# Block attention and a channel mixer on one core: in five of 32 pairs of heads, DMA transposes of halved probabilities in place of TensorE's

## The chip, the cores and the metric

The kernel runs on one core of a Trainium2 chip. Its engines work side by side, each through its own instructions in order: TensorE (PE; its weight loads are shown as PEld), VectorE (DVE), ScalarE (ACT), GpSimd (POOL) and SyncE (SP), which issues the DMA transfers. The metric is the device time of one execution in microseconds (us); less is better.

## What is computed

Eight batches of eight heads, 576 positions, 64 channels a head. Attention is masked by blocks of 64 positions, and its output goes through a mixer:

```python
scores = scale * np.matmul(q, k.transpose(0, 1, 3, 2))
mask = block_i >= block_j                    # blocks of 64 positions
attn = np.exp(scores - max) / (sum + 1e-09)
x = np.matmul(attn, v)                       # heads side by side: (8, 576, 512)
u = x + (x.transpose(0, 2, 1) @ U @ V).transpose(0, 2, 1)      # U: 576 x 32, V: 32 x 576
out = u + np.maximum(u @ w_ch1, 0.0) @ w_ch2                   # 512 x 2048, 2048 x 512
```

## The kernel before

Two heads are worked on together, so there are 32 pairs, four to a batch. The 576 rows of a head's scores lie in five blocks of rows: block 0 has 64 rows, blocks 1 to 4 have 128, and block i needs 128 i + 64 columns of keys. A pair is worked off in two sets of five such blocks (`scores(p, s, ...)` with s = 0 and 1; which block of which head belongs to which set is told by `job`). For each set PE makes the scores in PSUM (L1262), DVE finds the negative largest of each row (L1287), and ACT writes the exponentials to the tiles `p0_` to `p4_` in SBUF and their sums to `ss` (L1298). There are four tiles of each kind, taken by the number of the head.

`normalise` follows: DVE sums and inverts (L1311, L1312), and POOL multiplies the exponentials by the inverse in place (L1319). It also copies three small corners into neighbouring tiles.

The value product needs the probabilities with keys on the partitions, so `transpose` turns them on PE in squares of 128x128 in float32 (L1373), with the identity or a matrix that swaps the two halves (`swap`) as the other operand. The results go to PSUM and are copied from there to `pw` or `spare` by ACT (L1346), or, for one part in four from head 12 on, by DVE (L1344). `apply_v` (L1394) multiplies by V in float32: the queries lie in two groups of 256 and 320 columns (`g` = 1 and 0), with five and three blocks of keys; the two heads of a pair write the upper and lower 64 partitions of one bank. ACT copies the result to `xt`. `mix` then makes u of the pair (L1426, L1452, L1480), and DMA stores it in `u_d`.

The feed-forward part of the first 768 of the 2048 hidden channels is worked off in chunks of 288 positions, `ffn_chunk`: float32 numbers are split into a high and a low half-precision part, and three products (high by high, low by high, high by low) make one (L729 and L754). ACT and DVE copy its results out of two banks `bf`. These products run between those of the attention. The other 1280 channels come after the last pair, in `block_products` (L978).

All instructions are handed to `Plan` as tasks with an engine, a planned length, a priority, and what they read and write. `Plan.issue` plays the engines through with these planned lengths, always starting the ready task of lowest priority number on a free engine, and writes the instructions in that order. Attention of pair p has priorities around 2000 p (its scores some 2000 lower), feed-forward products 1e6 and up, and the copies that serve them -1. So PE takes a feed-forward product whenever, by the plan, no product of a pair is ready. The planned length of each task is varied by up to 2% with its number in the list, so that tasks added in one place also move later ones. On the chip each engine keeps the order that was written and waits by semaphores. A DMA is planned to land `DL` = 3000 ns after its issue.

SP issues every DMA, in the order of the plan: q and k of a pair (`raw`, L1210), V (`vr`, L1230), weights (`st`), u (`u_d`, `ur`) and the feed-forward results (`o_d`).

Of the kernel before, what the change touches and what calls it, by code (L numbers as in the profile page):

```python
# [189 lines left out]
class Plan:  # L190
# [140 lines left out]
def attention_then_mixer(  # L331
# [446 lines left out]
    def block_products():  # L778
# [29 lines left out]
        def at(x, *i):  # L808
            return lambda: first()[x][(slice(None), *i)]

        scored = after(*raw_r, xs, *usf.parts, *vf.parts)

        def weights(slots, by, sc, whole, room, split):

# [339 lines left out]
    ut_r = [b.split(2) for b in ring(ap, 1, [P, S], F32, "ut")]  # L1154
    ust = buf(ap, [P, 5, 2 * R], F32R, "ust").split(2)
    v3 = buf(ap, [3 * R, S], F32R, "v3").split(2)
    usf = buf(ep, [P, 5, R], F32, "usf").split(2)
    vf = buf(ep, [R, S], F32, "vf").split(2)
    xs = buf(ep, [P, 5, P], F32, "xs")


    for j in range(4):
# [142 lines left out]
    def normalise(p, s, pr):  # L1305
        slot = (2 * p + s) % 4
        ss, rv = ss_r[slot], rv_r[slot]

        def inverse():

            nc.vector.tensor_reduce(out=rv.ap, in_=ss.ap, op=ALU.add, axis=AX.X)  # L1311
            return nc.vector.reciprocal(rv.ap, rv.ap)  # L1312

        add("DVE", 274, pr, inverse, ss.parts, rv.parts)

        def scaled(out, x, iv, w, reads, to):
            add(
                "POOL", 255 + 0.85 * w, pr,
                lambda: nc.gpsimd.tensor_scalar(out=out, in0=x, scalar1=iv, scalar2=1.0, op0=ALU.mult, op1=ALU.mult),  # L1319
                reads, [to],  # L1320
            )

        def corner(q, h):
            r, n = rv_r[(2 * p + q) % 4], [i for _, i in job(p)].index(3)
            pt, to = pt_r[3][h % PB[3]], pt_r[4][h % PB[4]]
            scaled(to[0:64, 4 * P : 4 * P + 64], pt[64:P, 3 * P : 3 * P + 64], r[64:P, n : n + 1], 64, [r.parts[n], pt], to)

        for n, (x, i) in enumerate(job(p)):
            h = 2 * p + (s, 1 - s)[x]
            w, pt = P * i + 64, pt_r[i][h % PB[i]]  # L1330
            if i == 0:
                to = pt_r[1][h % PB[1]]
                scaled(to[0:64, P : P + 64], pt[0:64, 0:64], rv[0:64, n : n + 1], 64, [rv.parts[n], pt], to)
# [14 lines left out]
    def transpose(h, g, part, pr):  # L1348

        js = BLOCKS[g][part]  # L1350
        bank, span = Buf(pool=banks_p(h // 2)), _span(g, js)
        n = span.stop - span.start


        moves = []
        for j in js:
            for i in range(1, 5):
                q0 = max(P * i - 64, 0)
                a, b = max(q0, _first(g, j)), min(P * i + 64, QS[g + 1])
                if a < b and not (i == j == 3):  # L1360
                    c = _at(g, j).start - span.start + a - _first(g, j)
                    half = b - a < P
                    left = half and c + P > 512
                    moves.append((not half, i, j, swap if half and i and not left else ident, c - 64 if left else c))
        moves.sort(key=lambda m: m[0])

        def products():
            for _, i, j, perm, a in moves:
                to = bank[:, a : a + P]
                if i == j == 1 or j == 4:  # L1370
                    x, y = ((_at(g, n).start - span.start) // 64 for n in ((1, 0) if j == 1 else (3, 4)))
                    to = bank[:, :].rearrange("p (x c) -> p x c", c=64)[:, x : y + 1 : y - x, :]
                nc.tensor.transpose(out=to, in_=pt_r[i][h % PB[i]][:, j * P : (j + 1) * P], identity=perm.ap)  # L1373

        cost = 109 * len(moves)
        pts = [pt_r[i][h % PB[i]] for i in sorted({m[1] for m in moves})]
        pw = pw_of(h)[g]
        b = pw.parts[part]
        add("PE", cost, pr, products, pts, [bank], hold=[b])
        copy((g, part) in VEC and h >= 2 * VP, n, pr, lambda: pw[:, span], lambda: bank[:, :n], [bank], [b])  # L1380

    def apply_v(p, pr):
        xt, vr = xt_r[p % 2], vr_r[p % 2]
        pw = [[pw_of(2 * p + s)[g] for s in range(2)] for g in range(2)]
        bank = [Buf(pool=banks_p(p)) for _ in range(2)]
        n = [QS[g + 1] - QS[g] for g in range(2)]
        whole = [vr, *(y for g in pw for x in g for y in x.parts)]
        order = Buf()

        def products(g):  # L1390
            for j in range(NK[g]):
                x = max(P * j - QS[g], 0)
                for s in range(2):
                    nc.tensor.matmul(  # L1394
                        bank[g][64 * s : 64 * s + 64, x : n[g]], vr[:, 5 * s + j, :], pw[g][s][:, _at(g, j)],
                        start=(j == 0), stop=(j == NK[g] - 1),
                    )
# [128 lines left out]
    for p in range(NH // 2):  # L1526
        pr = 2000.0 * p
        if p + 1 < NH // 2:
            load_qk(p + 1, max(pr - LA, 1.0))
        for s in range(2):  # L1530
            scores(p, s, pr + 10 + 20 * s - (SL if p < NPAIR else SL2))
            normalise(p, s, pr + 30)
        for g in (1, 0):
            for h in (2 * p, 2 * p + 1):
                for part in range(2):
                    transpose(h, g, part, pr + 40 + 10 * (1 - g))
        apply_v(p, pr + 60)
        if p + 1 < NH // 2:
            load_v(p + 1, pr + 1000)
        mix(p, pr + (MX[1] if p % NPAIR == NPAIR - 1 else MX[0]))  # L1540
        if p == min(WH, NH // 2 - 1):
            gate = Buf()
            gate.writers = [len(plan.tasks) - 1]
            first_w2(lambda: wa, wab, lambda n: WPB + WP1 * n, 0, [gate])
            first_w1(lambda: wa, wab, lambda n: WP2 + WP3 * n, 1, [gate])
            first_w2(lambda: wa, wab, lambda n: WP4 + WP3 * n, 1, [gate])
# [55 lines left out]
```

## Time and profile before

| | before |
|---|---|
| time, median of three runs | 1076.9 us (1075.48 to 1077.45) |
| time of the profiled execution | 1076.24 us |
| its span, first to last instruction | 1074.4 us |
| granted clock | 1.000 |
| last value product of the attention | between 550 and 600 us |
| PSUM copies of the transposed probabilities and of `xt` on ACT (L1346) | 115.8 us, 268 instructions |
| scaling of the probabilities on POOL (L1319) | 183.5 us, 384 instructions |

The span runs from the first to the last instruction; the profiled execution's own time has 1.8 us around it. Busy time is given per engine; matmuls overlap in the pipeline, so that one of 288 columns is shown as 0.29 us long although the next starts 0.12 us after it. The time that a product costs is therefore read from the distance of starts, not from the length of one. The two parts of the table's last rows are whole lines over the span.

### The profile page before, as it was taken

The numbers are of one execution on the slowest core, as the hardware profiler recorded it, in microseconds if no ns is written. First come the engines' busy times: TensorE is split into PE (matmuls) and PEld (weight loads), VectorE is DVE, ScalarE is ACT, GpSimd is POOL, SyncE is SP. The second block draws the span as 40 slices with busy tenths as digits, with TensorE's granted clock in tenths as the row PEclk, the third lists the DMA queues.
The fourth block names the chain that finished last, engine by engine and source line by source line (L and its number), as shares of the span: only waits on it lengthen the run. The fifth ranks groups of instructions, "written<-read, shape, count | busy, mean of one in ns | idle before, by whom it ended". The sixth has DMA issues, their size and how long they took to land.

```text
span 1074.4 us, 25473 instructions
## 1 busy us (share of the span) xinstructions
PE 1065.3 (99%) x9676; PEld 845.8 (79%) x9676; DVE 850.3 (79%) x1799; ACT 650.7 (61%) x1674; POOL 346.3 (32%) x624
## 2 busy tenths in 40 slices
PE   9999999999999999999999999999999999999998
PEld 7678867888787888888877777777777777777776
DVE  5879987887764665778856643999898989999998
ACT  6888777766766667577585542545454545454553
POOL 4744436556545455365376460000000000000000
PEclk9999999999999999999999999999999999999999
DMA  4453635453433241444222422040404031313111
GB/s 146 136 175 121 201 107 186 137 174 116 130 103 101 82 131 63 151 132 160 89 80 74 127 59 75 1 126 9 133 13 122 18 116 32 103 37 98 41 50 45
DMA packets 68266, 107.37 MB, mean 100 GB/s; under 512 B 6896, under 2 KB 50928, under 8 KB 68144
## 3 DMA queue, kind: packets, MB, share of 16 engines
q1 hardware_dynamic: 68144, 105.75, 31.8%
q8 instruction: 76, 1.25, 0.5%
q14 instruction: 46, 0.38, 0.1%
HBM read 76.23 MB, written 29.49 MB: 98 GB/s over the span
## 4 chain that ended last, share of the span: by engine, by line
PE 93%; ACT 3%; DVE 2%; POOL 1%; issue 1%; DMA 0%; ACTq 0%; POOLq 0%; DVEq 0%
PE bb L978 38%; PE bf L754 13%; PE bf L729 12%; PE ba L1373 8%; PE ba L1394 8%; PE bw L1262 5%; PE bq L1262 3%; ACT p L1298 2%; PE ba L1426 2%; PE ba L1452 1%; PE ba L1480 1%; PE bf L1560 1%; POOL p L1319 1%; POOL w1l L831 0%; PE bf L1120 0%
## 5 line engine op out<-in xcount | busy, mean ns | idle before, releaser
L1319 POOL TENSOR_SCALAR p<-p,rv 64x64 f32<-64x64 f32 (+4 forms) x384 | 183.5, 490 | 111.1 <-DVE rv L1312 35.3
L978 PE MATMUL bb<-ph,w2h 128*128 128x288 f16 x560 | 151.1, 286 | 0.0
L978 PE MATMUL bb<-ph,w2l 128*128 128x288 f16 x560 | 151.1, 286 | 0.0
L978 PE MATMUL bb<-ph,w1l 128*128 128x288 f16 x560 | 148.8, 286 | 0.0
L978 PE MATMUL bb<-ph,w1h 128*128 128x288 f16 x560 | 148.8, 286 | 0.0
L900 ACT CAST ph<-hb 128x576 f16<-128x576 f32 x144 | 84.3, 589 | 83.1 <-PE bb L978 82.0
L978 PEld LDWEIGHTS <-w1h 128*128 128x128 f16 x1120 | 109.3, 98 | 28.0
L978 PEld LDWEIGHTS <-w2h 128*128 128x128 f16 x1120 | 109.3, 98 | 27.9
L978 PE MATMUL bb<-pl,w2h 128*128 128x288 f16 x560 | 123.7, 286 | 0.0
L1287 DVE TENSOR_REDUCE mx<-bw 128x1 f32<-128x576 f32 (+2 forms) x192 | 76.2, 436 | 50.1 <-PE bw L1262 49.2
L978 PE MATMUL bb<-pl,w1h 128*128 128x288 f16 x560 | 114.5, 286 | 0.0
L754 PE MATMUL bf<-hh,w2h 128*128 128x288 f16 x384 | 110.3, 287 | 0.4 <-DVE hl L737 0.4
L754 PE MATMUL bf<-hh,w2l 128*128 128x288 f16 x384 | 110.0, 286 | 0.6 <-DVE w2l L543 0.6
L754 PE MATMUL bf<-hl,w2h 128*128 128x288 f16 x384 | 109.9, 286 | 0.0
L1373 PE MATMUL ba<-ident,p 128*128 128x128 f32 x668 | 102.2, 276 | 0.0
L1298 ACT ACTIVATE p<-bw,mx 128x192 f32<-128x192 f32 (+2 forms) x192 | 92.5, 489 | 13.9 <-DVE mx L1287 12.0
L1262 PE MATMUL bw<-raw 64*64 64x288 f32 (+4 forms) x896 | 97.0, 346 | 0.4 <-ACT p L1298 0.3
L902 DVE TENSOR_TENSOR pl<-hb,ph 128x576 f16<-128x576 f32 x144 | 91.2, 650 | 1.5
L729 PEld LDWEIGHTS <-w1h 128*128 128x128 f16 x768 | 74.2, 98 | 19.9 <-issue 2.3
L1262 PE MATMUL bq<-raw 64*64 64x384 f32 (+1 forms) x496 | 89.7, 470 | 0.1
L754 PEld LDWEIGHTS <-w2h 128*128 128x128 f16 x768 | 75.1, 98 | 18.5 <-ACT w2h L539 0.2
L1373 PEld LDWEIGHTS ba<-ident,p 128*128 128x128 f32 x668 | 76.8, 141 | 5.6 <-issue 1.6
(193 smaller groups left out, 2386.5 us busy)
## 6 DMA issues: line engine op xcount, KB each, us to landing
raw<-in_qk_dram SPq DMA_DIRECT2D x31, 576.0 KB, 3.9
o_d<-ot SPq DMA_DIRECT2D x72, 144.0 KB, 1.8
vr<-in_v_dram SPq DMA_DIRECT2D x32, 320.0 KB, 3.0
ur<-u_d SPq DMA_DIRECT2D x64, 144.0 KB, 2.3
wr<-o_d SPq DMA_DIRECT2D x32, 288.0 KB, 3.1
out_dram<-wr SPq DMA_DIRECT2D x31, 288.0 KB, 2.3
st<-in_w_dram SPq DMA_DIRECT2D x16, 512.0 KB, 4.2
u_d<-ut SPq DMA_DIRECT2D x28, 288.0 KB, 2.1
```

The costliest lines, as they stand in the source:

```text
L729: nc.tensor.matmul(ps[:, :T], w()[wn][:, k, fs], m[k].ap, start=(i == 0), stop=(i == len(ops) - 1))
L754: nc.tensor.matmul(ps[:, :T], w()[wn][:, f, ms], hs[f][x].ap, start=(i == 0), stop=(i == len(ops) - 1))
L900: add("ACT", _act(n * T, True), E, lambda: nc.scalar.copy(h.ap[:, :n, :], x[0]()), [x[1]], [h])
L902: "DVE", _dve(n * T), E, lambda: nc.vector.tensor_sub(l.ap[:, :n, :], x[0](), h.ap[:, :n, :]), [x[1], h], [l],
L978: nc.tensor.matmul(bank[:, i, :T], x()[:, w(k)], p.ap[:, k, :], start=first and n == 0, stop=last and n == len(ops) - 1)
L1262: nc.tensor.matmul(o, raw[r, 64 * n : 64 * n + 64], raw[r, S + k0 : S + k1], start=True, stop=True)
L1287: lambda i=i, n=n: nc.vector.tensor_reduce(out=mx[: P if i else 64, n : n + 1], in_=view(i), op=ALU.max, axis=AX.XY if i == 4 else AX.X, n ...
L1298: return nc.scalar.activation(out.rearrange("p (j k) -> p j k", j=2) if i == 4 else out, view(i), AF.Exp, bias=mx[:rows, n : n + 1], accum ...
L1319: lambda: nc.gpsimd.tensor_scalar(out=out, in0=x, scalar1=iv, scalar2=1.0, op0=ALU.mult, op1=ALU.mult),
L1373: nc.tensor.transpose(out=to, in_=pt_r[i][h % PB[i]][:, j * P : (j + 1) * P], identity=perm.ap)
L1394: nc.tensor.matmul(bank[g][64 * s : 64 * s + 64, x : n[g]], vr[:, 5 * s + j, :], pw[g][s][:, _at(g, j)], start=(j == 0), stop=(j == NK[g] ...
L1426: nc.tensor.transpose(out=ps[:, i, :], in_=xt[:, j * P : j * P + rows], identity=ident.ap)
```

## The change

For the pairs 11, 15, 19, 23 and 27 (`XP`), two functions take the place of `normalise`, `transpose` and `apply_v`:

- `halve` scales the probabilities by 2^15 times the inverse sum and splits them into a high and a low half-precision part, side by side in one tile `hl16` for each kind of block. For blocks 0, 1 and 4, ACT makes the high part with the scaling in it (L1383) and DVE the low one; for blocks 2 and 3 (`XG`), POOL scales in place, ACT casts (L1379) and POOL subtracts. DMA transposes (`dma_start_transpose`, L1402) carry them into `turned`, keys on the partitions: one for blocks 2 and 4, two for the others, so eight a set and 16 a pair. There is one `hl16` tile of each kind, used by both sets, so that the second set's halves wait until the first set's transposes have read theirs. A transpose is planned with 600 ns on SP and a landing 8000 ns after (`XI`, `XD`).
- `apply_x` finds a power of two that brings V near a fixed size (DVE, with one transpose on PE), scales V on POOL, splits it into `vh` and `vl` on ACT and POOL, and multiplies in three half-precision passes (high by high, low by high, high by low): 48 products with a weight load each (L1434). ACT copies the result to `xt` with the inverse scale.

The tiles `turned` share their memory with three tiles that only the first four pairs use (`usf`, `vf`, `xs`).

```diff
+XP = (11, 15, 19, 23, 27)
+XI, XD = 600, 8000
+XG = (2, 3)
...
+    hl16 = [buf(ep, [P, 2, P * (i + 1)], F16, f"hl16_{i}") for i in range(5)]
+    vh, vl = (buf(ep, [P, 10, D], F16, x) for x in ("vh", "vl"))
...
+    def halve(p, s, pr):
...
+            if i in XG:
+                add(
+                    "POOL", 255 + 0.85 * w, pr,
+                    lambda x=x, iv=iv: nc.gpsimd.tensor_scalar(out=x, in0=x, scalar1=iv, scalar2=1.0, op0=ALU.mult, op1=ALU.mult),
+                    [rv.parts[n]], [pt],
+                )
+                add("ACT", _act(w, True), pr, lambda hi=hi, x=x: nc.scalar.copy(hi, x), [pt], [both])
+                add("POOL", 60 + 2.2 * w, pr, lambda hi=hi, lo=lo, x=x: nc.gpsimd.tensor_sub(lo, x, hi), [pt, both], [both])
+            else:
+                add(
+                    "ACT", _act(w, True) + 105, pr, lambda hi=hi, x=x, iv=iv: nc.scalar.activation(hi, x, AF.Copy, scale=iv),
+                    [rv.parts[n], pt], [both],
+                )
+                add(
+                    "DVE", 60 + 1.3 * w, pr,
+                    lambda hi=hi, lo=lo, x=x, iv=iv: nc.vector.scalar_tensor_tensor(
+                        out=lo, in0=x, scalar=iv, in1=hi, op0=ALU.mult, op1=ALU.subtract
+                    ),
+                    [rv.parts[n], pt, both], [both], port=True,
+                )
...
+            whole = i in (2, 4)
...
+            for n, (o, x) in enumerate(moves):
+                add(
+                    "SP", XI, pr, lambda o=o, x=x: nc.sync.dma_start_transpose(out=o, in_=x), [both],
+                    [] if n else [turn_b[side][i]], after=XD,
+                )
...
+    def apply_x(p, pr):
...
+            for j in range(NK[g]):
+                x = max(P * j - QS[g], 0)
+                for m, (v, a) in enumerate(((vh, 0), (vl, 0), (vh, 1))):
+                    for s in range(2):
+                        nc.tensor.matmul(
+                            bank[g][64 * s : 64 * s + 64, x : n[g]], v[:, 5 * s + j, :], turned[s][g][:, a, j, x:],
+                            start=(j == 0 and m == 0), stop=(j == NK[g] - 1 and m == 2),
+                        )
...
-            normalise(p, s, pr + 30)
...
+            (halve if p in XP else normalise)(p, s, pr + 30)
+        if p in XP:
...
+            apply_x(p, pr + 40)
+        else:
```

The order of the instructions is the same as before for about the first 100 us on every engine (apart from clearings of `hl16` on DVE) and for the last 6589 rows of PE; between these it is made anew. Three places follow, all of pair 15; line numbers are those of the kernel each piece is from.

On PE before, pair 15's value products end with group 0 (`pw_0`), and transposes of the next pair (`ident`) stand right behind:

```order
L1394 MATMUL ba_96<-pw_1_188,vr_192 64x64
L1394 MATMUL ba_96<-pw_1_190,vr_192 64x64
L1394 MATMUL ba_95<-pw_0_187,vr_192 64x320
L1394 MATMUL ba_95<-pw_0_189,vr_192 64x320
L1394 MATMUL ba_95<-pw_0_187,vr_192 64x192
L1394 MATMUL ba_95<-pw_0_189,vr_192 64x192
L1394 MATMUL ba_95<-pw_0_187,vr_192 64x64
L1394 MATMUL ba_95<-pw_0_189,vr_192 64x64
L1373 MATMUL ba_96<-ident,p_0_182 128x2x64
L1373 MATMUL ba_96<-ident,p_0_178 128x128
```

On PE with the change, the scores of pair 17 stand ahead, and the value products of pair 15 (`d_0` and `d_1` are the turned probabilities of its two heads) begin with a weight load for each:

```order
L1277 MATMUL bw<-raw_161 64x192
L1277 MATMUL bw<-raw_161 64x64
L1434 LDWEIGHTS vh
L1434 MATMUL ba_96<-d_0_213,vh 64x256
L1434 LDWEIGHTS vh
L1434 MATMUL ba_96<-d_1_214,vh 64x256
L1434 LDWEIGHTS vl
L1434 MATMUL ba_96<-d_0_213,vl 64x256
L1434 LDWEIGHTS vl
L1434 MATMUL ba_96<-d_1_214,vl 64x256
L1434 LDWEIGHTS vh
```

The 26 transposes of this pair are gone, and 48 products stand where 16 stood.

On ACT before, after the exponentials of pair 15's second set (`p2_2`), copies of transposes (`spare`) and casts of the mixing stand:

```order
L1298 ACTIVATE p2_2_176,ss3_165<-bq2_98,mx3_196 128x320
L1435 CAST xh0_203<-ba0_95 64x128
L1346 COPY spare_186<-ba1_96 128x512
L1346 COPY spare_186<-ba0_95 128x64
L1459 COPY tb0_207<-ba1_96 32x128
L1346 COPY spare_186<-ba0_95 128x512
L1461 CAST t3_0_205<-tz0_206 32x128
L1298 ACTIVATE p4_0_182,ss0_162<-bw_97,mx0_193 128x576
L1298 ACTIVATE p1_0_170,ss0_162<-bw_97,mx0_193 128x192
L1298 ACTIVATE p0_0_166,ss0_162<-bw_97,mx0_193 64x64
```

On ACT with the change, the halvings of the second set (`hl16`) stand at this place, each with a wait for a DMA (`DMAHW` with the number of the semaphore), since the first set's transposes read the same tiles; the exponentials of the next set stand behind them:

```order
L1313 ACTIVATE p2_2_176,ss3_165<-bq2_98,mx3_196 128x320 [waits DVE_49]
L1545 CAST xh0_203<-ba1_96 64x128 [waits PE_49]
L1383 ACTIVATE hl16_4_219<-p4_3_185,rv3_200 128x576 [waits DMAHW6_49,DVE_49,Activation_49]
L1383 ACTIVATE hl16_1_216<-p1_3_173,rv3_200 128x192 [waits DMAHW0_49,Activation_49]
L1569 COPY tb0_207<-ba1_96 32x128 [waits DVE_49,PE_49]
L1456 COPY spare_186<-ba0_95 128x512 [waits DVE_49,PE_49]
L1383 ACTIVATE hl16_0_215<-p0_3_169,rv3_200 64x64 [waits DMAHW2_49,Activation_49]
L1571 CAST t3_0_205<-tz0_206 32x128 [waits DVE_49]
L1313 ACTIVATE p4_0_182,ss0_162<-bw_97,mx0_193 128x576 [waits DVE_49]
L1456 COPY spare_186<-ba1_96 128x64 [waits PE_49]
```

On SP before, around the first store of u in batch 3 (`u_d3`):

```order
L1210 DMA raw0_160<-in_qk_dram 128x1152
L605 DMA st1_107<-in_w1_dram 128x640
L1503 DMA u_d3_77<-ut0_208 128x576
L605 DMA st0_106<-in_w1_dram 128x640
L774 DMA o_d1_83<-ot_137 128x288
L686 DMA ur1_126<-u_d2_76 128x288
L774 DMA o_d1_83<-ot_137 128x288
L686 DMA ur1_126<-u_d2_76 128x288
L1230 DMA vr1_192<-in_v_dram 128x640
```

On SP with the change, transposes of pair 15 (`hl16`) stand around this store, each behind its own waits, and the stores and loads of the feed-forward part (`o_d1`, `ur1`) stand between them:

```order
L1402 DMA_TRANSPOSE d0_0_211<-hl16_1_216 128x2x128 [waits Activation_49]
L1402 DMA_TRANSPOSE d0_0_211<-hl16_1_216 128x2x128 [waits DMAHW1_49,DVE_49]
L1402 DMA_TRANSPOSE d0_0_211<-hl16_0_215 128x1x64 [waits DMAHW2_49,Activation_49]
L1402 DMA_TRANSPOSE d0_0_211<-hl16_0_215 128x1x64 [waits DMAHW3_49,DVE_49]
L1613 DMA u_d3_77<-ut0_208 128x576 [waits DMAHW4_49,DVE_49]
L777 DMA o_d1_83<-ot_137 128x288 [waits DMAHW5_49,DVE_49]
L689 DMA ur1_126<-u_d2_76 128x288 [waits DMAHW6_49]
L1402 DMA_TRANSPOSE d1_1_214<-hl16_3_218 128x4x128 [waits DMAHW7_49,Activation_49]
L1402 DMA_TRANSPOSE d1_1_214<-hl16_3_218 128x4x128 [waits DMAHW0_49,Pool_49]
L777 DMA o_d1_83<-ot_137 128x288 [waits DMAHW1_49,DVE_49]
L689 DMA ur1_126<-u_d2_76 128x288 [waits DMAHW2_49]
L1402 DMA_TRANSPOSE d0_1_212<-hl16_2_217 128x6x128 [waits DMAHW3_49,Pool_49]
```

More of the change, by code (lines that the diff above doesn't have):

```diff
@@ L809, in at @@
             return lambda: first()[x][(slice(None), *i)]
-        scored = after(*raw_r, xs, *usf.parts, *vf.parts)
+        scored = after(*raw_r, xs, *usf.parts, *vf.parts, *hl16, vh, vl, *vs_r, *vi_r, *(b for r in turn_b for b in r))
         def weights(slots, by, sc, whole, room, split):
@@ L1156, in attention_then_mixer @@
     v3 = buf(ap, [3 * R, S], F32R, "v3").split(2)
-    usf = buf(ep, [P, 5, R], F32, "usf").split(2)
-    vf = buf(ep, [R, S], F32, "vf").split(2)
-    xs = buf(ep, [P, 5, P], F32, "xs")
+    dt0, dt1 = ([ep.tile([P, n], F32, name=f"d{g}_{x}") for x in range(2)] for g, n in ((0, 960), (1, 1280)))
+    usf = Buf(dt1[1][:, : 5 * R].rearrange("p (j r) -> p j r", j=5)).split(2)
+    vf = Buf(dt0[0][:R, :S]).split(2)
+    xs = Buf(dt1[0][:, : 5 * P].rearrange("p (j d) -> p j d", j=5))
+    turned = [
+        [t[x][:, :].bitcast(F16).rearrange("p (a j q) -> p a j q", a=2, j=j) for t, j in ((dt0, 3), (dt1, 5))] for x in range(2)
+    ]
+    turn_b = [[Buf() for _ in range(5)] for _ in range(2)]
+    hl16 = [buf(ep, [P, 2, P * (i + 1)], F16, f"hl16_{i}") for i in range(5)]
+    vh, vl = (buf(ep, [P, 10, D], F16, x) for x in ("vh", "vl"))
+    vs_r, vi_r = ring(ep, 2, [P, 2], F32, "vs"), ring(ep, 2, [P, 1], F32, "vi")
+    mv_r = [b.split(1) for b in ring(ep, 2, [P, 1], F32, "mv")]
     for j in range(4):
@@ L1167, in attention_then_mixer @@
             nc.vector.memset(p[:, P * i + 64 :], 0.0)
+    for i, b in enumerate(hl16):
+        nc.vector.memset(b[:, :, P * i + 64 :], 0.0)
     def mixing_weights(prio):
@@ L1340, in normalise, with inverse @@
             corner(1, 2 * p)
+    def halve(p, s, pr):
+        slot = (2 * p + s) % 4
+        ss, rv = ss_r[slot], rv_r[slot]
+        def inverse():
+            nc.vector.tensor_reduce(out=rv.ap, in_=ss.ap, op=ALU.add, axis=AX.X)
+            nc.vector.reciprocal(rv.ap, rv.ap)
+            return nc.vector.tensor_scalar(out=rv.ap, in0=rv.ap, scalar1=2.0 ** 15, scalar2=1.0, op0=ALU.mult, op1=ALU.mult)
+        add("DVE", 340, pr, inverse, ss.parts, rv.parts)
+        for n, (x, i) in enumerate(job(p)):
+            side = (s, 1 - s)[x]
+            h, w, rows, both = 2 * p + side, P * i + 64, P if i else 64, hl16[i]
+            pt, iv = pt_r[i][h % PB[i]], rv[:rows, n : n + 1]
+            hi, lo, x = both[:rows, 0, :w], both[:rows, 1, :w], pt[:rows, :w]
+            if i in XG:
[18 more added lines that the diff above has]
+                )
+            g, q = (0, max(P * i - 64, 0)) if i < 3 else (1, P * i - 64 - QS[1])
+            to = turned[side][g]
+            whole = i in (2, 4)
+            if whole:
+                moves = [(to.rearrange("p a j q -> p (a j) q")[:, :, q : q + rows], both[:rows, :, :].rearrange("p a k -> p (a k)"))]
+            else:
+                moves = [(to[:, a, : i + 1, q : q + rows], both[:rows, a, :]) for a in range(2)]
+            for n, (o, x) in enumerate(moves):
[3 more added lines that the diff above has]
+                )
+                if n:
+                    turn_b[side][i].writers.append(len(plan.tasks) - 1)
@@ new lines, in apply_x, with products @@
+    def apply_x(p, pr):
+        xt, vr = xt_r[p % 2], vr_r[p % 2]
+        sc, iv, mu = take(vs_r, "vs"), take(vi_r, "vi"), take(mv_r, "mv")
+        largest(lambda: vr.ap.rearrange("p a b -> p (a b)"), 10 * D, vr, mu, 0, pr)
+        power(mu, 1, 2.0 ** 6, sc, pr, banks_p(p))
+        add(
+            "DVE", 70, pr,
+            lambda: nc.vector.tensor_scalar(out=iv.ap, in0=sc[:, 1:2], scalar1=2.0 ** -28, scalar2=1.0, op0=ALU.mult, op1=ALU.mult),
+            [sc], [iv], port=True,
+        )
+        add(
+            "POOL", 145 + 0.85 * 10 * D, pr,
+            lambda: nc.gpsimd.tensor_scalar(out=vr.ap, in0=vr.ap, scalar1=sc[:, 0:1], scalar2=1.0, op0=ALU.mult, op1=ALU.mult), [sc], [vr],
+        )
+        add("ACT", _act(10 * D, True), pr, lambda: nc.scalar.copy(vh.ap, vr.ap), [vr], [vh])
+        add("POOL", 60 + 2.2 * 10 * D, pr, lambda: nc.gpsimd.tensor_sub(vl.ap, vr.ap, vh.ap), [vr, vh], [vl])
+        bank = [Buf(pool=banks_p(p)) for _ in range(2)]
+        n = [QS[g + 1] - QS[g] for g in range(2)]
+        whole = [vh, vl, *(b for r in turn_b for b in r)]
+        order = Buf()
+        def products(g):
+            for j in range(NK[g]):
[5 more added lines that the diff above has]
+                            start=(j == 0 and m == 0), stop=(j == NK[g] - 1 and m == 2),
+                        )
+        for g in (1, 0):
+            cost = 3 * sum(5 + 0.4167 * max(n[g] - max(P * j - QS[g], 0), 60) for j in range(NK[g]))
+            add(
+                "PE", cost + PVX * g, pr if g else -1e5, lambda g=g: products(g), [*whole, *([] if g else [order])],
+                [bank[g], *([order] if g else [])], hold=xt.parts,
+            )
+        for g in (1, 0):
+            add(
+                "ACT", _act(n[g]) + 105, pr,
+                lambda g=g: nc.scalar.activation(xt[:, QS[g] : QS[g + 1]], bank[g][:, : n[g]], AF.Copy, scale=iv.ap),
+                [bank[g], iv], [xt.parts[g]],
+            )
@@ L1531, in attention_then_mixer @@
             scores(p, s, pr + 10 + 20 * s - (SL if p < NPAIR else SL2))
-            normalise(p, s, pr + 30)
[L1533 to L1537, printed above, removed]
+            (halve if p in XP else normalise)(p, s, pr + 30)
+        if p in XP:
+            if p == XP[0]:
+                for b in (b for r in turn_b for b in r):
+                    for x in (xs, *usf.parts, *vf.parts):
+                        b.readers += x.readers + x.writers
+            apply_x(p, pr + 40)
+        else:
+            for g in (1, 0):
+                for h in (2 * p, 2 * p + 1):
+                    for part in range(2):
+                        transpose(h, g, part, pr + 40 + 10 * (1 - g))
+            apply_v(p, pr + 60)
         if p + 1 < NH // 2:
```

## The prediction

> **What bounds the kernel now.** I read the page first: busy shares, then the chain that ended last, then the busy time by stage.
>
> ```profile
> PE 1065.3 (99%) x9676; PEld 845.8 (79%) x9676; DVE 850.3 (79%) x1799; ACT 650.7 (61%) x1674; POOL 346.3 (32%) x624
> ...
> PE 93%; ACT 3%; DVE 2%; POOL 1%; issue 1%; DMA 0%; ACTq 0%; POOLq 0%; DVEq 0%
> ```
>
> PE is busy for all but 9 us of the 1074.4 us span, and the chain runs on PE for 93% of it. Since a busy PE need not be a necessary PE, I ask whether there is other PE work to move up where the change takes some away. The stages say so (columns: length, then busy PE, PEld, DVE, ACT, POOL, each with its instructions, clock, DMA share, GB/s):
>
> ```profile
> 140.00:160.00 20.00, 18.70 (x181) 13.47 (x181) 16.14 (x49) 16.24 (x46) 6.47 (x14) 1.00 0.35 100
> ...
> 200.00:250.00 50.00, 50.00 (x501) 40.60 (x500) 43.36 (x111) 36.32 (x117) 27.27 (x53) 1.00 0.46 144
> 250.00:300.00 50.00, 49.99 (x495) 39.92 (x496) 36.08 (x92) 37.60 (x110) 30.59 (x59) 1.00 0.45 137
> ...
> 400.00:450.00 50.00, 50.00 (x497) 40.45 (x497) 31.99 (x84) 32.32 (x109) 24.41 (x49) 1.00 0.29 94
> ```
>
> From 200 us on PE is full. The same view of single lines tells with what: the second feed-forward product (L754) at 250 and at 600 us, and the pairs' value products (L1394) at 600 us:
>
> ```profile
> 250.00:300.00 50.00, 12.86 (x94) 8.88 (x91) 1.00 0.45 137
> 600.00:650.00 50.00, 24.65 (x199) 19.14 (x196) 1.00 0.25 74
> ...
> 600.00:650.00 50.00, 0.00 (x0) 0.00 (x0) 1.00 0.25 74
> ```
>
> Feed-forward products fill the gaps between the pairs, and after the last pair many are left. So PE time removed from an attention pair is taken by a product that stood later, and the end comes forward by that time, if no new wait opens. The five pairs lie in this stage. A pair's value products leave 32 records, and their line counts
>
> ```profile
> 350.00:400.00 50.00, 8.81 (x96) 6.11 (x96) 1.00 0.32 102
> ```
>
> 96 in 50 us, three pairs, so 16.7 us a pair.
>
> **What PE loses and gains.** Transposes before, and the value products of a pair, by the timeline (start, length, engine, group):
>
> ```profile
> 0.00:600.00 600.00, 126.40 (x832) 94.34 (x832) 1.00 0.41 129
> ...
> 340.86 0.48 PEld L1373 LDWEIGHTS ba<-ident,p 128*128 128x128 f32 x4
> 340.98 0.60 PE L1373 MATMUL ba<-ident,p 128*128 128x128 f32 x4
> ...
> 343.80 0.29 PE L754 MATMUL bf<-hl,w2h 128*128 128x288 f16 x1
> 344.01 2.94 PE L1394 MATMUL ba<-spare,vr 128*64 128x256 f32 x32
> ...
> 346.88 0.66 PE L1373 MATMUL ba<-ident,p 128*128 128x128 f32 x4
> ...
> 351.75 0.27 PE L1373 MATMUL ba<-swap,p 128*128 128x128 f32 x1
> ```
>
> 832 transposes are 26 a pair. Four start within 0.60 us less the 0.27 us of one, so the pitch is 0.11 us, and a pair's transposes cost 26 x 0.11 = 2.86 us. Its value products hold PE from 344.01 to 346.88, 2.87 us. Both go.
>
> In their place stand 48 half-precision products (8 blocks, 3 passes, 2 heads) with a weight load each. No row shows such a product with 64 columns of weights; the nearest are the wide feed-forward ones and the idle fillers:
>
> ```profile
> L1560 PEld LDWEIGHTS <-zero x20: 97/98/98, 72.2 to 74.1; 128*128 128x128 bf16 x20
> L1560 PE MATMUL bf<-zero x20: 218/220/220, 72.3 to 74.2; 128*128 128x128 bf16 x20
> ...
> 72.15 0.65 PEld L1560 LDWEIGHTS <-zero 128*128 128x128 bf16 x10
> 72.26 0.72 PE L1560 MATMUL bf<-zero 128*128 128x128 bf16 x10
> ...
> 353.03 0.66 PE L729 MATMUL bf<-uh,w1h 128*128 128x288 f16 x4
> ```
>
> Four of 288 columns start 0.12 us apart, (0.66 - 0.29) / 3, which is 0.43 ns a column. The ten fillers start within 0.72 - 0.22 = 0.50 us, 0.056 us a product with its load. The two heads write different halves of the bank's partitions and run side by side: before, 1600 columns a head in 2.87 us are 1.8 ns a column, four times the 0.43, not eight. If columns alone count, three passes take 3 x 1600 x 0.43 = 2.1 us. If every product also pays the filler's pitch, a couple of heads takes at least 0.112 us, except the 320-column one at 0.138: 3 x (7 x 0.112 + 0.138) = 2.77 us. If no load hides, 48 x 0.098 (the median of one load) = 4.7 us. I take 2.75, by the nearest row, and keep 2.1 and 4.7. Added as well is one transpose in finding the scale of V, 0.11 us. A pair then saves 2.86 + 2.87 - 2.75 - 0.11 = 2.87 us of PE, five pairs **14.3 us**; the bounds are 17.6 (at 2.1) and 4.6 (at 4.7).
>
> [...]
>
> **What the other engines get.** Groups of instructions; behind the bar the busy us and the mean ns of one:
>
> ```profile
> L1319 POOL TENSOR_SCALAR p<-p,rv 64x64 f32<-64x64 f32 (+4 forms) x384 | 183.5, 490 | 111.1 <-DVE rv L1312 35.3
> L900 ACT CAST ph<-hb 128x576 f16<-128x576 f32 x144 | 84.3, 589 | 83.1 <-PE bb L978 82.0
> ...
> L1346 ACT COPY pw<-ba 128x64 f32<-128x64 f32 (+1 forms) x113 | 50.8, 461 | 20.4 <-PE ba L1373 16.7 <-DVE mx L1287 1.7 <-DVE pw L1344 0.5
> L713 POOL TENSOR_TENSOR ul<-us,uh 128x288 f16<-128x288 f32 x56 | 40.1, 731 | 28.0 <-ACT uh L712 13.2 <-DVE spare L831 3.3 <-ACT ph L907 3.0
> ...
> L912 DVE SCALAR_TENSOR_TENSOR pl<-ur,sc,ph 128x576 f16<-128x576 f32 x42 | 34.1, 813 | 2.3 <-ACT ph L907 2.3
> L907 ACT ACTIVATE ph<-ur,sc 128x576 f16<-128x576 f32 x42 | 32.6, 775 | 26.2 <-PE bb L978 26.2
> ...
> L712 ACT CAST uh<-us 128x288 f16<-128x288 f32 x56 | 22.8, 435 | 7.0 <-POOL us L707 5.5 <-PE bf L729 1.2
> ...
> L1344 DVE COPY pw<-ba 128x512 f32<-128x512 f32 x32 | 21.8, 685 | 5.5 <-PE ba L1373 4.9 <-ACT tb L1459 0.3
> ```
>
> ACT loses six copies of 0.46 us a pair (2.8) and gains ten halvings: 0.78 for 576 columns, about 0.52 and 0.45 for 448 and 320 (between 435 and 589), 0.4 and 0.35 for the small ones (estimates from the same rows), twice, and 0.62 for V: 5.6. That is +2.8 us a pair. DVE loses two copies (1.4) and gains six low parts (2 x (0.81 + 0.4 + 0.25) = 2.9), the largest of V over 640 columns (0.8 by the 685 for 512) and some ten small ones of 0.15 to 0.28 (1.7): about +4.0. POOL loses 12 scalings (5.9) and gains four scalings (2.0), four subtractions at 731/288 = 2.5 ns a column (3.9) and V's two (0.7 + 1.6): +2.3. Per 16.7 us, ACT was busy 10.8 in the stage at 400 us and comes to 13.6 (81%), DVE 10.7 and 14.7 (88%), POOL 8.1 and 10.4.
>
> No engine becomes the bound, but PE waits more often when its partners are that full: 140 to 160 us, with DVE at 81% and ACT at 81%, PE lost 1.3 us of 20. Five pairs, 84 us, at that rate lose 5.5 us; at the rate of the stage from 200 us they lose nothing. With an order made anew from some 100 us on I take **2.3 us**, near the middle. Two edits cost nothing: five more clearings on DVE before the first scores exist, and five more idle fillers within the first 130 us, where PE has nothing else to do.
>
> **The transposes.** A pair issues 16 of them, 60 blocks of 128x128 or less. No transfer of this kind is in the trace. The rows from issue to landing, and the time of an issue on SP, are
>
> ```profile
> o_d<-ot SPq DMA_DIRECT2D x72, 144.0 KB, 1.8
> vr<-in_v_dram SPq DMA_DIRECT2D x32, 320.0 KB, 3.0
> ...
> st<-in_U_dram SPq DMA_DIRECT2D x1, 128.0 KB, 5.9
> ...
> 272.14 0.33 SPq L1210 DMA_DIRECT2D raw<-in_qk_dram  x1
> ...
> 298.24 0.53 SPq L686 DMA_DIRECT2D ur<-u_d  x1
> ```
>
> The largest moves 320 KB, so 1.8 to 5.9 us bound its landing from below and from the nearest rows; how far above it may lie, nothing here says. What is allowed can be read: on ACT the first halving of a pair's second set of blocks stands, in pair 15, 21 rows behind that of the first set and waits for its landing, as both share a tile. 1674 ACT records stand for 1340 rows of its order, and 110 of them fill 50 us at 250 us, so 21 rows are about 12 us. The halving, the low part and the issue take 0.78 + 0.81 + 0.33 of that; with the queue, some **9 us** are left for the landing. At the bounds' 1.8 to 5.9 it is hidden and costs nothing. I take 5, hidden. Behind the waiting instruction on ACT stand exponentials and the copies that free PE's banks; on PE, behind the waiting value product, feed-forward products and scores; on SP, behind a transpose that waits for its halves, the loads of q, k, v and u.
>
> [...]
>
> **The sum.** Against the profiled execution's 1076.2 us: 1076.2 - 14.3 + 2.3 = 1064.2. That execution lies 0.7 below the median of the three, 1076.9, so for the median I say **1065**.
>
> **The rivals.**
> *Crowded partners.* ACT at +2.8 and DVE at +4.0 us a pair delay the copies that free PE's banks at the full rate of 140 to 160 us: 5.5 instead of 2.3, 1068. For it speaks that row; against it, that 200 to 250 us shows DVE at 87% with PE full.
> *Late landing (the other side).* If a transpose lands later than the 9 us, ACT stops at the second set's halving and PE once more at the value products: at most 2 us a pair for each us, 10 us in all. The gain of 12 is eaten at 10.2 us of landing; at 11 us the time is 1065 + 20 = 1085. For it speaks that the kind is unseen and that two sets share a tile; against it, that every landing in the trace is under 6.
> *Issue by block.* If SP spends 0.33 us on each of the 60 blocks, it is held 20 us a pair, where nine issues in the 26 us between the two rows leave it about 14 of 16.7 free. Loads behind fall 5 us late a pair, PE starves as much: 1065 + 26 = 1091. [...]
> *It doesn't free PE.* With no weight load hidden (4.7 us), 4.6 instead of 14.3 go: 1065 + 9.7 = 1075, no change that shows.
>
> **How the numbers follow.** Forecast 0.60 (1058 to 1070: the bound 17.6 without waits, 5 us more waits), crowded 0.12, late landing 0.15, issue by block 0.08, PE not freed 0.05. Range **1058 to 1086**: all of the first two and the last, and the late landing up to 11 us. About 0.2% (2.2 us) is what a measurement of this kernel can tell from no change. Faster: 0.60 + 0.12, and 0.02 of the others; same: 0.06, mostly PE not freed; slower: 0.20.
>
> **What would show it.** PE's 48 products within 2.1 to 2.8 us, with no transposes in five pairs; landing of a transpose under 9 us; ACT's halvings idle before them for no DMA; PE idle between 200 and 550 us under 4 us. Wrong I am if ACT or PE shows waits of microseconds for transposes, or if SP's issues run to over a microsecond each.

## The result and the profile after

| | before | after |
|---|---|---|
| time, median of four runs | 1076.19 us (1075.32 to 1077.45) | 1088.68 us (1087.30 to 1089.16) |
| time of the profiled execution | 1076.24 us | 1088.98 us |
| its span | 1074.4 us | 1087.2 us |
| span less PE's busy time | 9.1 us | 30.0 us |
| granted clock | 1.000 | 0.989 |

The ratio is 1.0113, with a 95% interval of 1.0096 to 1.0131: slower, and above the top of the range. The granted clock is the profile's figure for TensorE's clock as a share of its full speed. The lines of the page after the change follow: busy time by engine, the granted clock in 40 slices of the span (9 is 90% or more), and the chain that ended last. That chain is followed back only to 418 us, so its shares can't be set against those of before.

```profile
PE 1057.2 (97%) x9636; PEld 837.1 (77%) x9636; DVE 864.3 (79%) x1874; ACT 661.3 (61%) x1699; POOL 362.4 (33%) x614
PEclk9999999999899998998999999999999999999999
PE 57%; ACT 1%; DMA 1%; POOL 1%; issue 1%; DVE 1%; SPq 0%; POOLq 0%; ACTq 0%; DVEq 0%
```

PE was busy 8.1 us less and idle 20.9 us more, which makes the 12.8 us of span. The clock, at full speed throughout before, is under 90% in three slices. Where that happens the windows of after tell (length, then busy PE, PEld, DVE, ACT, POOL, each with its instructions, clock, DMA share, GB/s): the whole stage with the five pairs, and the four stretches of 20 us in it where PE lost most.

```profile
200.00:550.00 350.00, 328.89 (x3292) 262.11 (x3290) 246.01 (x644) 232.54 (x724) 187.59 (x338) 0.97 0.54 142
200.00:220.00 20.00, 15.68 (x133) 11.78 (x134) 12.41 (x34) 11.96 (x39) 10.31 (x19) 0.91 0.75 186
280.00:300.00 20.00, 15.92 (x151) 11.66 (x151) 8.72 (x25) 11.79 (x39) 12.76 (x22) 0.83 0.56 153
420.00:440.00 20.00, 15.92 (x131) 11.25 (x125) 10.45 (x29) 9.10 (x31) 8.42 (x14) 0.83 0.52 132
500.00:520.00 20.00, 14.05 (x119) 10.54 (x119) 9.09 (x29) 9.65 (x31) 12.10 (x19) 0.83 0.84 183
```

Of before, the same stage reads

```profile
200.00:550.00 350.00, 349.64 (x3484) 282.70 (x3484) 250.80 (x634) 239.69 (x748) 183.76 (x359) 1.00 0.37 119
```

So all 21 us of new idle time lie between 200 and 550 us, 18.4 of them in the four stretches; DVE and ACT are less busy there too, and POOL 4 us more, so no engine took PE's place as the bound. What the partners wait for is in the list of waits (who waits, for what; us in total, times, longest). Before:

```profile
POOL raw L1220 <- DMA raw<-in_qk_dram: 27.3, 9, 8.4
ACT z L439 <- DMA st<-in_w_dram: 4.7, 5, 1.8
```

After:

```profile
POOL raw L1235 <- DMA raw<-in_qk_dram: 37.0, 12, 6.0
ACT z L442 <- DMA st<-in_w_dram: 22.5, 7, 7.5
POOL us L710 <- DMA ur<-u_d: 12.3, 3, 6.1
```

ACT's wait for weights (`st`) grew by 17.8 us, POOL's for q, k and u by 22. None of the long waits is for a transpose. Once issued, the loads take little longer in the median: 3.7 us to landing for the `st` of 512 KB (4.2 before), 4.4 for q and k (3.9 before). Of those behind which PE stalls, two do: q and k issued at 271.59 us land after 6.4 us, and the `st` issued at 499.84 after 7.3. The timeline of after at the first stall (start, length, engine, group; in brackets the idle time before it) shows how the loads come to be late:

```profile
186.30 2.62 SPq L1402 DMA_TRANSPOSE d<-hl  x2
...
190.12 8.71 SPq L1402 DMA_TRANSPOSE d<-hl  x6
198.93 0.52 SPq L1613 DMA_DIRECT2D u_d<-ut  x1
199.88 0.34 SPq L608 DMA_DIRECT2D st<-in_w_dram  x1
...
200.80 0.38 SPq L608 DMA_DIRECT2D st<-in_w_dram  x1
201.28 3.88 SPq L1402 DMA_TRANSPOSE d<-hl  x3
205.25 0.53 SPq L1225 DMA_DIRECT2D raw<-in_qk_dram  x1
...
204.03 0.48 ACT L442 ACTIVATE z<-st 128x320 f32<-128x320 f32 x1 [5.14 <-DMA st<-in_w_dram]
...
205.02 0.69 DVE L1548 TENSOR_TENSOR xl<-ba,xh 128x512 fp32r<-128x512 f32 x1 [4.56 <-ACT xh L1545]
...
207.05 0.65 PE L732 MATMUL bf<-uh,w1h 128*128 128x288 f16 x4 [4.33 <-DVE hl L740]
```

Six transposes hold SP for 8.71 us, three more for 3.88. The first weights behind the six are issued at 199.88 and land at 203.94; ACT, which works in order, stands still for 5.14 us and converts them at 204.03; DVE waits for ACT's next cast, and PE for DVE. The stalls that end at 283, 427 and 511 us are of the same kind: at 283 POOL had waited for `raw` (ACT at the same time for `st`, 7.50 us), at 427 POOL for `raw`, at 511 ACT for `st`. The line of the transposes says what one costs (ns: least, median, most; then us from issue to landing):

```profile
L1402 SPq DMA_TRANSPOSE d<-hl x80: 1114/1218/4124, 186.3 to 516.5; - x80
...
DMA to landing us min/median/max: 2.3/2.8/8.1
```

The 80 rows of the timeline add up to 111 us, 22 us a pair, where the plan has 16 x 0.6 = 9.6. And the new value products, in the windows of their line (PE, PEld, clock, DMA share, GB/s):

```profile
200.00:230.00 30.00, 2.26 (x48) 2.08 (x48) 0.94 0.66 181
280.00:300.00 20.00, 2.26 (x48) 2.08 (x48) 0.83 0.56 153
...
510.00:530.00 20.00, 2.26 (x48) 2.09 (x48) 0.88 0.66 187
```

They take 2.26 us in four of the pairs, 2.45 in the fifth. A second loss shows when the stall at 281 us is cut into windows of 2 us:

```profile
278.00:280.00 2.00, 2.00 (x16) 1.46 (x16) 1.02 (x2) 0.00 (x0) 1.90 (x3) 1.00 1.03 281
280.00:282.00 2.00, 0.03 (x1) 0.00 (x0) 0.00 (x0) 0.00 (x0) 2.00 (x4) 1.00 0.22 20
282.00:284.00 2.00, 0.96 (x4) 0.67 (x5) 0.00 (x0) 0.00 (x0) 0.99 (x3) 0.67 0.82 258
284.00:286.00 2.00, 0.97 (x5) 0.32 (x4) 0.76 (x2) 1.38 (x4) 0.45 (x1) 0.50 1.12 193
286.00:288.00 2.00, 2.00 (x9) 1.15 (x10) 2.00 (x8) 1.48 (x5) 0.80 (x1) 0.50 1.12 269
288.00:290.00 2.00, 2.00 (x13) 1.34 (x11) 0.56 (x3) 1.00 (x3) 0.00 (x0) 0.62 0.78 280
290.00:292.00 2.00, 2.00 (x23) 1.73 (x22) 1.00 (x3) 1.95 (x8) 0.92 (x2) 1.00 0.38 152
```

The clock stays at half for some 6 us after the stall's end: PE, where it counts as busy there, does half as much. Feed-forward products of 288 columns start 0.24 us apart there (five starts from 288.22 to 289.18 us), and 0.12 before the stall (five from 278.64 to 279.13).

### The profile page after: what moved, and what is told of

It reads as the page before. It is cut to its first block, busy times and chain, and to the rows that moved or that the text cites. A ratio compares the mean times of both kernels' runs of the same rounds, so it can differ in the third digit from the quotient of the medians.

```text
span 1087.2 us, 25617 instructions
## 1 busy us (share of the span) xinstructions
PE 1057.2 (97%) x9636; PEld 837.1 (77%) x9636; DVE 864.3 (79%) x1874; ACT 661.3 (61%) x1699; POOL 362.4 (33%) x614
## 2 busy tenths in 40 slices
DMA packets 107948, 116.90 MB, mean 108 GB/s; under 512 B 46576, under 2 KB 90608, under 8 KB 107824
## 3 DMA queue, kind: packets, MB, share of 16 engines
q1 hardware_dynamic: 107824, 115.26, 37.6%
## 4 chain that ended last, share of the span: by engine, by line
PE 57%; ACT 1%; DMA 1%; POOL 1%; issue 1%; DVE 1%; SPq 0%; POOLq 0%; ACTq 0%; DVEq 0%
PE bb L981 38%; PE bf L757 6%; PE bf L732 6%; PE ba L1483 2%; PE ba L1504 1%; PE bw L1277 1%; PE bq L1277 1%; DMA st<-in_w_dram 1%; PE ba L1536 1%; POOL p L1334 0%; PE ba L1562 0%; PE ba L1590 0%; PE ba L1434 0%; DMA ur<-u_d 0%; ACT p L1313 0%
## 5 line engine op out<-in xcount | busy, mean ns | idle before, releaser
L1334 POOL TENSOR_SCALAR p<-p,rv 128x576 f32<-128x576 f32 (+2 forms) x324 | 156.1, 495 | 84.7 <-DVE rv L1327 19.3
L981 PEld LDWEIGHTS <-w2h 128*128 128x128 f16 x1120 | 109.6, 98 | 27.7
L1313 ACT ACTIVATE p<-bw,mx 128x192 f32<-128x192 f32 (+2 forms) x192 | 92.7, 490 | 25.3 <-DVE mx L1302 24.8
L1483 PE MATMUL ba<-ident,p 128*128 128x128 f32 x558 | 84.3, 274 | 2.1 <-ACT xt L1456 1.3
L1277 PEld LDWEIGHTS bw<-raw 64*64 64x64 f32 x896 | 65.4, 134 | 18.2 <-issue 5.6
```

Of the source, the lines that this page charges most:

```text
L981: nc.tensor.matmul(bank[:, i, :T], x()[:, w(k)], p.ap[:, k, :], start=first and n == 0, stop=last and n == len(ops) - 1)
L1277: nc.tensor.matmul(o, raw[r, 64 * n : 64 * n + 64], raw[r, S + k0 : S + k1], start=True, stop=True)
L1313: return nc.scalar.activation(out.rearrange("p (j k) -> p j k", j=2) if i == 4 else out, view(i), AF.Exp, bias=mx[:rows, n : n + 1], accum ...
```

## The experiments

My theory after this reading: the time for which SP is held by the issues delays the loads behind them, and nothing else about the transposes matters. Against it stood the traffic (58% more packets, 107824 against 68144 on the DMA queue, or the way a transpose moves them), and the new order of instructions itself. Each ratio below is to the kernel before, run beside it (medians 1076.25 for the first four and 1076.57 for the last three).

**Copies in place of transposes.** The same tiles, order and bytes, only not turned (and the smallest tile cleared whole at the start):

```diff
-                moves = [(to.rearrange("p a j q -> p (a j) q")[:, :, q : q + rows], both[:rows, :, :].rearrange("p a k -> p (a k)"))]
+                moves = [(to.rearrange("p a j q -> p (a j) q")[:, :, q : q + rows], both[:, :, :].rearrange("p a (k q) -> p (a k) q", q=P))]
...
-                    "SP", XI, pr, lambda o=o, x=x: nc.sync.dma_start_transpose(out=o, in_=x), [both],
+                    "SP", XI, pr, lambda o=o, x=x: nc.sync.dma_start(out=o, in_=x), [both],
```

> The 16 DMA transposes of a pair become plain copies of the same bytes between the same tiles, so what the value products read is not the transposed probabilities; the order of every engine is that of the change. Theory 1 (a transpose holds SP 1.2 us, loads queued behind it go out late, ACT and POOL wait for them in their own order and PE starves): plain issues take 0.33 to 0.55 us, so the waits on loads of weights and q, k vanish, PE's idle time goes from 30 us back to about 10, time 1062 to 1070. Theory 2 (the packets of the transposes crowd the 16 DMA engines, so loads land late): the packets stay, time stays 1084 or more. Theory 3 (the new order alone is bad): time stays 1084 or more.

1060.48 us (1059.49 to 1061.37), ratio 0.9852 [0.9838, 0.9867], a little under the range expected. Its page, and the lines of the issues and of the same stretch of SP:

```profile
PE 1048.2 (99%) x9636; PEld 834.1 (79%) x9636; DVE 865.7 (82%) x1874; ACT 661.1 (62%) x1699; POOL 362.2 (34%) x614
...
q1 hardware_dynamic: 107824, 115.26, 36.1%
```

```profile
L1404 SPq DMA_DIRECT2D d<-hl x80: 497/610/1916, 186.9 to 488.9; - x80
```

```profile
189.61 4.70 SPq L1404 DMA_DIRECT2D d<-hl  x6
195.15 0.33 SPq L1615 DMA_DIRECT2D u_d<-ut  x1
195.90 0.34 SPq L608 DMA_DIRECT2D st<-in_w_dram  x1
...
198.47 0.38 SPq L608 DMA_DIRECT2D st<-in_w_dram  x1
```

With the same number of packets and bytes the whole loss is gone, so neither the order nor the amount of traffic makes it by itself. Nor is it the landing: q and k land after 4.5 us in the median here, after 4.4 with transposes. The six issues hold SP for 4.70 us instead of 8.71, and the first of the weights goes out at 195.90 instead of 199.88. This run also splits the 27.7 us by which the profiled execution of after is longer (1088.98 - 1061.26). Both kernels have the same 9636 products. Here PE is busy 1048.2 us and idle 1059.5 - 1048.2 = 11.3; after, 1057.2 and 30.0. So 18.7 us are idle time and 9.0 are the same products at a lower clock: by the clock records of after, PE is busy for 17.5 us at half the clock, which loses 8.7.

**Transposes of one small square.** In four of the five pairs each transpose carries a block of 64x128 only:

```diff
-                    "SP", XI, pr, lambda o=o, x=x: nc.sync.dma_start_transpose(out=o, in_=x), [both],
+                    "SP", XI, pr, lambda o=o, x=x: nc.sync.dma_start_transpose(
+                        out=o if p == XP[0] else o[:, :1, :64], in_=x if p == XP[0] else x[:64, :P]
+                    ), [both],
```

> In four of the five pairs (15, 19, 23, 27) each transpose moves only its first 64 rows by 128 columns, so most of the turned probabilities there are stale; count and order of the issues are those of the change. Theory 1: if the 1.2 us belong to an instruction whatever its size, nothing changes: 1084 to 1090. Theory 2: most of the packets are gone, four fifths of the lost time comes back: 1066 to 1073. Theory 3: 1084 or more.

1079.52 us (1074.00 to 1081.80 in ten runs), ratio 1.0020 [1.0006, 1.0034]. The line of the issues:

```profile
L1402 SPq DMA_TRANSPOSE d<-hl x80: 1088/1177/2129, 186.6 to 504.3; - x80
```

A transpose of one small block holds SP for 1.18 us in the median, one of up to ten squares 1.22: the cost is mainly one of the instruction, not of its blocks. But 9 us came back, where I had expected none. The issues of up to 4.1 us are gone (now 2.1 at most), the sum on SP is 100 us instead of 111, and in the timeline the stall of 4.08 us at 427 us is now one

```profile
420.42 0.53 PE L1592 MATMUL ba<-v,t 96*128 96x288 f32 x2 [2.03 <-POOL t L1574]
```

of 2.03 us, after which the clock stays at 1.00.

**Fewer, larger transposes.** The tiles are widened to three or five squares, and one transpose carries both halves of a block of rows: ten a pair instead of 16.

```diff
-    hl16 = [buf(ep, [P, 2, P * (i + 1)], F16, f"hl16_{i}") for i in range(5)]
+    hl16 = [buf(ep, [P, 2, P * (3 if i < 3 else 5)], F16, f"hl16_{i}") for i in range(5)]
...
+            one = (to.rearrange("p a j q -> p (a j) q")[:, :, q : q + rows], both[:rows, :, :].rearrange("p a k -> p (a k)"))
...
+                    "SP", XI, pr, lambda n=n, one=one: None if n else nc.sync.dma_start_transpose(out=one[0], in_=one[1]), [both],
```

> One transpose a block instead of two for blocks 0, 1 and 3 (their tiles widened with zeros to three or five squares), 10 a pair instead of 16; same order otherwise. Theory 1: SP is held 13 us a pair instead of 20, a good half of the waits goes: 1072 to 1082. Theory 2: the bytes grow by about a third, same or slower: 1087 to 1095. Theory 3: 1084 or more.

1063.39 us (1062.20 to 1064.63), ratio 0.9882 [0.9866, 0.9899]: better than I had expected.

```profile
L1403 SPq DMA_TRANSPOSE d<-hl x50: 1191/1342/2446, 185.7 to 490.3; - x50
```

The bytes are more than after (117.23 MB on the queue against 115.26), the issues 72 us in all, 14.3 a pair, and of the stalls of 0.9 us and more two are left, of 1.35 and 0.99 us. The copies had held SP for 53 us, 10.6 a pair, with one of 1.11 us; so in this order the loads' slack is used up between the 14.3 us a pair of these and the 22 of the change.

**The plan told what a transpose costs.** The same 80 transposes; only the planned issue and landing change, and with them the order.

```diff
-XI, XD = 600, 8000
+XI, XD = 1280, 3000
```

> Only the plan's figures for a transpose are changed, to what was measured: 1280 ns on SP instead of 600, landing 3000 ns after instead of 8000. The order is made anew. Theory 1: loads are put where SP can issue them in time, 1064 to 1076. Theory 2: SP's order matters little, 1083 or more. Theory 3: a draw of the order, anywhere from 1070 to 1090, with no fewer waits on loads.

1069.70 us (1067.82 to 1071.15), ratio 0.9937 [0.9923, 0.9952]. SP is held nearly as long as after (106 us in all), but only one stall over 2 us is left, 3.69 us at 293 us. ACT's waits for `st` fall from 22.5 us to 12.8 and POOL's for `ur` from 12.3 to 0.3; those for q and k grow from 37.0 to 42.9. Whether the new figures did this or merely another draw of the order, one run of the plan does not tell.

**Copies issued in two halves.** The first experiment again, each copy as two of 64 partitions: no transposes, the bytes of the first experiment, but 32 issues a pair.

```diff
-                    "SP", XI, pr, lambda o=o, x=x: nc.sync.dma_start(out=o, in_=x), [both],
+                    "SP", XI, pr, lambda o=o, x=x: [nc.sync.dma_start(out=o[r], in_=x[r]) for r in (slice(0, 64), slice(64, P))], [both],
```

> As the run with plain copies, but each copy is issued as two of 64 partitions: the same bytes, no transposes, 32 issues a pair in place of 16 (the value products again read copies, not transposes). Theory 1 (the time that SP is held): SP is held some 18 to 21 us a pair, as by the transposes, and the waits on loads and the lost time come back: 1078 to 1090. If something of the transposes themselves were at fault: 1060 to 1064, as with whole copies.

1089.25 us (1087.88 to 1089.41), ratio 1.0120 [1.0105, 1.0136]: the time of the change, without a single transpose. Line of the issues, and windows:

```profile
L1404 SPq DMA_DIRECT2D d<-hl x160: 461/602/2182, 186.7 to 517.3; - x160
```

```profile
200.00:550.00 350.00, 329.67 (x3292) 262.92 (x3291) 246.09 (x645) 232.10 (x724) 186.87 (x338) 0.97 0.49 142
200.00:220.00 20.00, 15.13 (x120) 11.35 (x119) 11.51 (x32) 11.02 (x37) 9.29 (x17) 0.83 0.71 175
...
420.00:440.00 20.00, 15.56 (x132) 11.01 (x133) 9.12 (x27) 8.58 (x26) 7.81 (x14) 0.83 0.54 136
```

The 160 issues hold SP for 102 us, 20 a pair, and the stalls are back, in the same stretches and with like dips of the clock. This run and the first differ in the number of issues, and so in the time on SP (and by 1% of the packets); with the change it shares that time, and not the kind of transfer. So it is the time on SP that makes the loads late.

**The weights from another queue.** The change as it is, but ACT issues the loads of the weights, so that they don't stand behind the transposes:

```diff
-                    [lambda s, src=src: nc.sync.dma_start(out=s, in_=src.rearrange("p (n t) -> p n t", t=2))], [P, HB // 2],
+                    [lambda s, src=src: nc.scalar.dma_start(out=s, in_=src.rearrange("p (n t) -> p n t", t=2))], [P, HB // 2],
```

> The change as it is, transposes and their plan included, but the loads of the last 1280 channels' weights are issued on ACT's queue, so that they no longer stand behind transposes; the order of the other instructions is that of the change. Theory 1: ACT's waits on these loads (22.5 us) fall to under 8 us, the stalls of PE near 203, 282 and 507 us go or shrink, those on the loads of q and k near 424 us stay: 1070 to 1080. If the lateness of these loads had been hidden anyway: 1086 to 1090.

1079.95 us (1074.85 to 1081.93 in ten runs), ratio 1.0021 [1.0004, 1.0037]. Waits, and windows:

```profile
POOL raw L1235 <- DMA raw<-in_qk_dram: 53.0, 14, 6.7
...
POOL us L710 <- DMA ur<-u_d: 16.5, 4, 5.4
...
ACT z L442 <- DMA st<-in_w_dram: 8.8, 10, 1.6
```

```profile
200.00:220.00 20.00, 20.00 (x219) 16.20 (x217) 15.54 (x41) 14.97 (x50) 15.42 (x28) 1.00 0.95 181
...
420.00:440.00 20.00, 15.20 (x120) 10.41 (x122) 8.88 (x27) 8.42 (x29) 8.69 (x14) 0.83 0.52 128
500.00:520.00 20.00, 20.00 (x205) 15.81 (x205) 15.99 (x45) 14.41 (x49) 12.69 (x20) 1.00 0.96 179
```

The two stalls behind weights, at 200 and 500 us, are gone, with the same transposes on SP. ACT's waits for weights fall from 22.5 us to 8.8, a little above the 8 expected. The stall behind `raw` at 420 us stays, since q, k and u still queue behind transposes, and the waits for these grow (37.0 to 53.0 us for q and k). And a new one opens:

```profile
275.67 0.35 ACTq L608 DMA_DIRECT2D st<-in_w_dram  x1
276.12 0.46 ACT L1379 CAST hl<-p 128x320 f16<-128x320 f32 x1 [5.42 <-DMA d<-hl]
276.90 0.32 PE L487 MATMUL ba<-ident,oneu 128*128 128x128 f32 x1 [3.73 <-ACT xt L1456]
```

The load's issue now stands in ACT's own order. By the trace's semaphores it waits for a transpose (issued at 268.62 us, landed at 275.59), and ACT's halving, its copy to `xt` and PE stand behind it. So the issues brought their own wait into the order of the engine that took them.

**Both remedies.** Ten transposes a pair, planned with 1430 ns and a landing of 4000 ns (the widened tiles as above, and `XI, XD = 1430, 4000`).

> Ten transposes a pair as before, and the plan told what they take: 1430 ns on SP, landing 4000 ns after. Theory 1: at or below the 1063.4 of ten transposes with the old figures: 1058 to 1064. If what was left there was the draw of the order, it may come out anywhere from 1060 to 1070.

1059.49 us (1058.48 to 1059.91), ratio 0.9845 [0.9831, 0.9860]. Faster than both kernels, with PE busy for all but 9.8 us of its span of 1056.7.

```profile
PE 1046.9 (99%) x9636; PEld 832.9 (79%) x9636; DVE 862.3 (82%) x1874; ACT 661.7 (63%) x1699; POOL 359.1 (34%) x614
```

## Why the prediction was wrong

- **The failing step is that of the transposes.** It asked when they land, took 5 us, and called them hidden; for their issue it used the 0.33 us of a plain transfer, and the sum held nothing for SP. The landing was right: 2.8 us in the median, 8.1 at most, under the 9 us allowed, and no halving on ACT waited for one. What cost the time is that each of the 80 instructions holds SP for 1.22 us in the median, 22 us a pair, in bursts of up to 9.8 us (seven in a row), with loads behind them. Against the run with copies that cost 27.7 us.
- **What PE saves** was sized at 14.3 us; PE's busy time fell by 1065.3 - 1048.2 = 17.1 us in the run with copies, just inside the bound of 17.6. The term taken too high was the 48 products: 2.26 us and not 2.75, near the bound of 2.1 that counts columns alone.
- **PE's waits on fuller partners**, 2.3 us in the sum: in the run with copies PE is idle 11.3 us, 2.2 more than before. The size came out; that fuller partners are its cause isn't shown, and with both remedies, where they are as full, it is 0.7. Per pair ACT, DVE and POOL grew busier by 2.1, 2.8 and 3.2 us, where the prediction had 2.8, 4.0 and 2.3.
- **The rivals.** *Issue by block* named the right engine and place, and its 1091 is near the 1088.7, but it had a chance of 0.08, and the nearness is luck in part, since its mechanism was off twice. The cost goes by instruction and not by block (1.18 us for one small block, 1.34 for six and ten squares). And its price of 26 us was all starvation, where 18.7 us are that and 9.0 are the clock that falls after long stalls, which no step foresaw. *Crowded partners*, *Late landing* and *It doesn't free PE* fell: 2.2 us of waits, a landing in time, and 17.1 us freed. The argument against a late landing, that every landing of before is under 6 us, holds for the medians of the rows only: single ones took 7.2 us (`st`) and 6.3 (`raw`).
- **The range** ended at 1086 because it left out *Issue by block*, and because the issue time of an unseen instruction was bounded by rows of plain transfers alone. The same prediction had "SP's issues run to over a microsecond each" among what would make it wrong; a bound at that value, 16 x 1 us a pair against some 14 free, would have shown the queue full.
- **What stays open**: why single issues stretch to 4.1 us when large transposes follow one another, and to 2.1 at most with small ones, no run here shows. Nor does the sum on SP alone set the time, so "nothing else matters" was too strong: 20 us a pair cost 19 us over the run with copies with small transposes (1079.5), 28.8 with halved copies (1089.3), and 21 us a pair in the order of the other plan cost 9.2 (1069.7). Which loads stand behind a burst, and how long the stalls become, must count as well, though no run changed that alone; the part on the clock says why the length matters.

## What to carry to other kernels

A transfer has two prices, the landing (2.8 us in the median for the transposes here) and the time for which its issue holds the queue (1.22 us); multiply the second by the number in a burst and hold it against the gaps of that queue, also where the landing is hidden. Of the 28.2 us between the change and the run with copies, fewer, larger transposes won back 25.3, the plan with the measured times 19.0, and the weights on another queue 8.7; the first two together took the ratio from 1.011 to 0.985. Each of the 13 stalls of PE of 3.01 to 5.95 us here had a mean granted clock of 0.59 to 0.79 in the 8 us behind it; such a stall is to be counted with its aftermath at half the clock.

## What was unexpected of the hardware

**The issue of a transpose.** 1.18 us for a block of 64x128, 1.22 for the mixture of the change (up to ten squares), 1.34 for six and ten squares: almost a constant, about twice a plain copy of the same tiles (0.61) and nearly four times a plain load (0.33). In these runs the median grows by 0.16 us from the small block to six and ten squares, so at such sizes the instruction's own cost decides.

**The clock after a stall.** All stalls of PE of 0.9 us and more between 180 and 600 us, in the kernel after and the experiments, with the granted clock of the 8 us from the whole microsecond before their end (the timeline gives the stall, the windows the clock):

| stall | how many | clock of the 8 us behind |
|---|---|---|
| 0.93 to 1.67 us | 12 | 1.00 in all |
| 2.03, 2.07, 2.34 us | 3 | 1.00, 0.79, 1.00 |
| 3.01 to 5.95 us | 13 | 0.59 to 0.79 |

(A thirteenth short stall stands within the slow stretch at 286 us and is left out.) The clock halves (0.50 in the windows at 284 and 286 us). By the clock records of after it is at half in four stretches of the stage, of 3.4, 6.8, 6.8 and 6.8 us, one at each of its four stalls of 3 us and more. Near 2 us the length of a stall alone doesn't tell whether this comes: behind 2.07 us it came, behind 2.03 and 2.34 it did not, and behind 3.01 us and more it always did; what else decides, no run here shows. So a loss of this kind isn't proportional: the 1.35 us stall of the merged transposes cost its length (clock 1.00 behind it), the 3 us one at 283 us its length and some 3 us more (5.4 us busy at half the clock).
